# Expert blocks of 128 tokens laid between the tiles of a top-k attention

## Chip, cores and metric

One core of one Trainium2 chip. The metric is the device time of one execution in microseconds; lower is better.

## What is computed

The first stage is attention over 8 batches, 8 heads, 576 positions and head size 64, in which every query keeps only its 32 best scores. Its output, 4608 tokens of 512 numbers, goes through a layer of 8 experts, of which each token uses one. Everything is float32.

```python
scores = scale * np.matmul(q, k.transpose(0, 1, 3, 2))        # (8, 8, 576, 576)
kth = np.partition(scores, -top_k, axis=-1)[..., -top_k:-top_k + 1]
scores = np.where(scores >= kth, scores, -1000000000.0)
attn = softmax(scores)                                        # top_k = 32
x = np.matmul(attn, v).transpose(0, 2, 1, 3).reshape(4608, 512)
logits = x @ w_gate                                           # (4608, 8)
expert_idx = np.argmax(logits, axis=1)
gate_w = probs[np.arange(N), expert_idx]                      # softmax of logits
y[tokens of e] = np.maximum(x[tokens of e] @ w1[e], 0.0) @ w2[e]   # 512 -> 1024 -> 512
out = gate_w[:, None] * y
```

## The kernel before

**Attention.** The work list (`work`) runs over 8 batches, 4 units a batch (a unit is two heads, 128 rows of transposed q and k) and 5 groups a unit: 160 groups. A group is two tiles of 128 queries, one of each head (groups 0 to 3), or one tile that holds the last 64 queries of both heads (group 4); a unit has 9 tiles. For a tile TensorE makes 576 scores per query (`scores`, L213), ScalarE copies them to `s` (L219), and VectorE finds the 32 largest (`weights`): it folds the row into 288 maxima and 288 minima (`hl`, L223 and L224), runs MAX8 four times with three MATCH_REPLACE8 between them over the maxima and MAX8 once over the minima, and merges both into a threshold. GpSimd makes the bias of the exponential (`nbias`, L247), ScalarE the exponential (L249), and VectorE the masked weights `w` and their row sum (L277). `transposed` turns `w` (TensorE L289, L290; ScalarE copies L294, L295); after group 4 `outputs` multiplies by v (L321), turns the result and scales it into `x` (VectorE L330, L337). Groups are software pipelined: scores of group n+1 are issued ahead of the weights of group n, and those ahead of the transposes of group n-1. Within that the framework's scheduler sets each engine's order when the program is built; at run time every engine takes its instructions strictly in that order.

**Routing.** After each second batch `route` works on its 1152 tokens: it turns all of `x` (L350, ScalarE copy L352), multiplies by the gate weights (L354), takes the best expert with small VectorE operations, counts each token's place in its expert's list by two matmuls (L370, L371), scatters token numbers into the lists in DRAM by nine indirect DMAs from GpSimd's queue (L393), each of which waits for the one before, and writes `x` to `x_rows` in DRAM.

**Experts.** After all attention `table` lays the lists out as 25 slots of 256 tokens (18 full ones and up to 7 more, since each expert's last slot is partly empty). A new set of pools is opened. For a slot `load_slot` reads the token numbers and 4 MB of weights (L155, L157; three buffers, two slots ahead) and gathers 256 rows of `x_rows` on GpSimd's queue (L470); `block` turns them (TensorE L482, VectorE copy L483), multiplies by w1 (L488: 128-column weights of TensorE, 256 tokens streaming), applies the rectifier on ScalarE (L491), multiplies by w2 (L495: 512 columns streaming), scales on VectorE (L499) and scatters the rows to the output (L500). In the trace one float32 matmul of the source is two TensorE instructions, each with its own weight load (PEld); a transpose is one.

PSUM has 8 banks: in the attention 4 for scores, 2 for `wTm`, 1 for `wTl` and `xtr`, 1 for `po`, `px`, `pl`, `lg`, `rank`. At the end a run-time branch repeats everything by an exact method if a query's threshold is in doubt; it is not taken here.

Of the kernel before, what the change touches and what calls it, by code (L numbers as in the profile page):

```python
# [26 lines left out]

def _back(ap: bass.AP) -> bass.AP:
# [6 lines left out]
def _inner(ap: bass.AP, n: int) -> bass.AP:  # L35
    return _ins(ap, len(ap.ap), n)


@with_exitstack
def kernel(  # L40
    ctx: ExitStack,
    tc: tile.TileContext,
    qt: bass.AP,
    kt: bass.AP,
    vt: bass.AP,
# [25 lines left out]

    nc = tc.nc
    B, HD, S = qt.shape
# [3 lines left out]
    P = 128  # L77
    D = 64
    U = HD // P
# [6 lines left out]
    NP = B // 2  # L86
# [3 lines left out]
    BLK = 256  # L90
    CB = BLK // P
    EB = N // BLK
    NSLOT = EB + E - 1
    LIST = E * N
    assert ST == 64 and Dm == HD and N == B * S and B % 2 == 0
    assert N % BLK == 0 and LIST % P == 0 and TOP_K == 32 and Dm == 512
    scale = float(D) ** -0.5

# [4 lines left out]
    lists = dram.tile([LIST, 1], I32, name="lists")  # L103
# [10 lines left out]
    nc.sync.dma_start(wg, moe_w_gate.rearrange("(t p) e -> p t e", p=P))  # L114

# [9 lines left out]
    blocks = iota_f("blocks", [1, EB], [[BLK, EB]])  # L125
    slots = iota_f("slots", [1, NSLOT], [[1, NSLOT]])

    def token_ids(t, p):
        b0 = 2 * p * S
        nc.gpsimd.iota(t[:, 0:NC], pattern=[[P, NC]], base=b0, channel_multiplier=1)  # L130
        nc.gpsimd.iota(t[:, NC:2 * NC], pattern=[[P, NC]], base=b0 + S, channel_multiplier=1)
        nc.gpsimd.iota(t[0:ST, 2 * NC:NT], pattern=[[1, 1]], base=b0 + SM, channel_multiplier=1)
        nc.gpsimd.iota(t[ST:P, 2 * NC:NT], pattern=[[1, 1]], base=b0 + S + SM, channel_multiplier=1)

    tok_id = []
    for p in range(NP):
# [12 lines left out]

    w1v = moe_w1.rearrange("e (dt p) f -> p e dt f", p=P)  # L150
    w2v = moe_w2.rearrange("e (ft p) d -> p e ft d", p=P)

    def load_w(pool, e):
        w1 = pool.tile([P, 1, DT, F], F32, name="w1")
        nc.sync.dma_start(w1, w1v[:, bass.ds(e, 1), :, :])  # L155
        w2 = pool.tile([P, 1, FT, Dm], F32, name="w2")
        nc.sync.dma_start(w2, w2v[:, bass.ds(e, 1), :, :])  # L157
        return w1, w2

    firstp = ctx.enter_context(tc.tile_pool(name="firstp", bufs=1))  # L160
# [3 lines left out]
    qk, vs_of, xt, units = {}, {}, {}, {}  # L164

    def open_pools(st, load_bufs, exact):
        for name, bufs in (
            ("load", load_bufs), ("att", 2), ("wtp", 2), ("xp", 1), ("small", 3),
        ):
            setattr(k, name, st.enter_context(tc.tile_pool(name=name, bufs=bufs)))  # L170
        for name, bufs in (("ps_s", 2), ("ps_w", 2), ("ps_1", 1)):
# [3 lines left out]
        k.cnt = None  # L175
        k.ntop = 0
        k.late = None

    def load_qk(b, u, at=None):
        at = b if at is None else at  # L180
        qb = k.load.tile([P, 2, S], F32, name="qb")
        nc.sync.dma_start(qb, qt[at, u * P:(u + 2) * P, :].rearrange("(u p) s -> p u s", p=P))
        kb = k.load.tile([P, 2, S], F32, name="kb")
        nc.sync.dma_start(kb, kt[at, u * P:(u + 2) * P, :].rearrange("(u p) s -> p u s", p=P))
        for n in range(2):
            qk[b, u + n] = (qb[:, n, :], kb[:, n, :])

    def load_v(b, at=None):
        at = b if at is None else at
        vb = k.load.tile([P, KC, HD], F32, name="vb")  # L190
        nc.sync.dma_start(vb[:, 0:NC, :], vt[at, 0:SM, :].rearrange("(c p) d -> p c d", p=P))
        nc.sync.dma_start(vb[0:ST, NC, :], vt[at, SM:S, :])
        vs_of[b] = vb
# [8 lines left out]
    def scores(b, u, tiles):  # L202
        qu, ku = qk[b, u]
# [6 lines left out]
        for j in range(2):  # L210
            for ps, h, rows, cols in todo:
                d = slice(h * D, (h + 1) * D)
                nc.tensor.matmul(  # L213
                    ps[rows, j, 0:HF], qu[d, cols], ku[d, j * HF:(j + 1) * HF], start=True, stop=True
                )
        out_s = []
        for ps in got:
            s = k.att.tile([P, 2, HF], F32, name="s", bufs=4)
            nc.scalar.copy(s, ps[:, :, 0:HF])  # L219
            hl = None  # L220
            if not k.exact:
                hl = k.att.tile([P, 2, HF], F32, name="hl", bufs=4)
                nc.vector.tensor_tensor(hl[:, 0, :], s[:, 0, :], s[:, 1, :], op=ALU.max)  # L223
                nc.vector.tensor_tensor(hl[:, 1, :], s[:, 0, :], s[:, 1, :], op=ALU.min)  # L224
            out_s.append((s, hl))
        return out_s

    def weights(b, u, tiles, ss):
        n = len(tiles)
        s = [a[:, :, :].rearrange("p j k -> p (j k)") for a, _ in ss]  # L230
        tops = tops_of[k.ntop % NTOP]
        k.ntop += 1
        nbias = k.small.tile([P, 2], F32, name="nbias")
        ex = [k.att.tile([P, S], F32, name="ex", bufs=4) for _ in tiles]
        if k.exact:
            src = list(s)
            width = S
        else:
            src = [hl[:, 0, :] for _, hl in ss]
            width = HF  # L240
        scr = [k.att.tile([P, width], F32, name="scr", bufs=3) for _ in tiles]
        R = TOP_K // 8
        for r in range(R):
            for m in range(n):
                nc.vector.max(out=tops[:, m, r * 8:(r + 1) * 8], in_=src[m])  # L245
            if r == 0:
                nc.gpsimd.tensor_scalar(nbias[:, 0:n], tops[:, 0:n, 0], -scale, None, ALU.mult)  # L247
                for m in range(n):
                    nc.scalar.activation(ex[m], s[m], AF.Exp, scale=scale, bias=nbias[:, m:m + 1])  # L249
                if not k.exact:  # L250
                    for m in range(n):
                        nc.vector.max(out=tops[:, m, TOP_K + 1:TOP_K + 9], in_=ss[m][1][:, 1, :])
            if r < R - 1:
                for m in range(n):
                    nc.vector.match_replace(  # L255
                        out=scr[m], in_to_replace=tops[:, m, r * 8:(r + 1) * 8],
                        in_values=src[m], imm_value=NEG,
                    )
                    src[m] = scr[m]
        z = units[b, u][2]  # L260
        i = tiles[0]
        c = 2 * NC if i == 2 * NC else 2 * i
        if k.exact:
            thr = tops[:, :, TOP_K - 1]
        else:
            both = k.small.tile([P, 2, 9], F32, name="both")
            nc.vector.tensor_tensor(
                both[:, 0:n, :], _back(tops[:, 0:n, TOP_K - 9:TOP_K]), tops[:, 0:n, TOP_K:TOP_K + 9], op=ALU.min
            )
            thr = k.small.tile([P, 2], F32, name="thr")  # L270
            nc.vector.tensor_reduce(thr[:, 0:n], both[:, 0:n, :], axis=AX.X, op=ALU.max)  # L271
            over = units[b, u][3]
            nc.gpsimd.tensor_tensor(over[:, c:c + n], tops[:, 0:n, TOP_K + 8], thr[:, 0:n], op=ALU.subtract)
        ws = []
        for m in range(n):
# [372 lines left out]
```

## Time and profile before

| | |
|---|---|
| time, median of 3 runs | 2424.38 us (2403.55 to 2433.43) |
| time of the profiled execution | 2420.5 us, span 2418.8 us |
| TensorE, VectorE, ScalarE, GpSimd busy | 74%, 61%, 29%, 11% of the span |
| granted TensorE clock, mean | 0.785 |
| DMA traffic | 167.0 MB |

The span falls into two stages. In the first, VectorE is nearly always busy and TensorE is busy about two thirds of the time at a clock that changes between its two levels; in the second TensorE is busy all the time at full clock and VectorE hardly at all. Busy times of TensorE include the drain of each matmul, so a high share is not peak use.

### The profile page before, as it was taken

The numbers are of one execution on the slowest core, as the hardware profiler recorded it, in microseconds if no ns is written. First come the engines' busy times: TensorE is split into PE (matmuls) and PEld (weight loads), VectorE is DVE, ScalarE is ACT, GpSimd is POOL, SyncE is SP. The second block draws the span as 40 slices with busy tenths as digits, with TensorE's granted clock in tenths as the row PEclk, the third lists the DMA queues.
The fourth block names the chain that finished last, engine by engine and source line by source line (L and its number), as shares of the span: only waits on it lengthen the run. The fifth ranks groups of instructions, "written<-read, shape, count | busy, mean of one in ns | idle before, by whom it ended". The sixth has DMA issues, their size and how long they took to land. (4 is left out here: it accounts for less than half of the span.)

```text
span 2418.8 us, 23413 instructions
## 1 busy us (share of the span) xinstructions
PE 1781.4 (74%) x7210; PEld 1099.0 (45%) x7210; DVE 1487.1 (61%) x5087; ACT 694.8 (29%) x1457; POOL 257.2 (11%) x486
## 2 busy tenths in 40 slices
PE   5756667666666765666775666662999999999998
PEld 3333335333333533333543333342666666666665
DVE  8899988799999699999769998930000010011000
ACT  3333434344344344443333433410111111111110
POOL 1011000200000011000011100002111111111110
PEclk9677766667766667676657767655999999999999
DMA  4001001100000200100110000014454544445530
GB/s 151 20 2 38 20 1 40 40 20 20 20 20 20 59 21 1 40 21 0 40 40 20 20 1 0 1 39 166 175 174 177 188 172 170 172 172 177 176 127 2
DMA packets 71191, 167.00 MB, mean 69 GB/s; under 512 B 9612, under 2 KB 9740, under 8 KB 71058
## 3 DMA queue, kind: packets, MB, share of 16 engines
q1 hardware_dynamic: 61906, 142.83, 17.6%
q0 software_dynamic: 9152, 22.60, 2.4%
q8 instruction: 59, 0.97, 0.2%
q14 instruction: 74, 0.61, 0.1%
HBM read 146.34 MB, written 22.73 MB: 70 GB/s over the span
## 5 line engine op out<-in xcount | busy, mean ns | idle before, releaser
L289 PE MATMUL wTm<-ident,w 128*128 128x128 f32 x1152 | 265.7, 374 | 492.9 <-DVE w L277 490.6
L289 PEld LDWEIGHTS wTm<-ident,w 128*128 128x128 f32 x1152 | 194.8, 196 | 568.4 <-issue 541.9
L213 PE MATMUL sc<-kb,qb 64*128 64x288 f32 (+1 forms) x1280 | 401.7, 586 | 42.9 <-ACT s L219 35.8
L249 ACT ACTIVATE ex<-s,nbias 128x576 f32<-128x576 f32 x288 | 209.6, 769 | 602.0 <-POOL nbias L247 602.0
L488 PE MATMUL ph<-xTs,w 128*128 128x256 f32 x1600 | 352.7, 381 | 14.1 <-DVE xTs L483 14.1
L245 DVE MAX8 tops<-scr 128x8 f32<-128x288 f32 x864 | 354.4, 446 | 0.1
L495 PE MATMUL py<-w,hT 128*128 128x512 f32 x800 | 347.4, 592 | 0.0
L488 PEld LDWEIGHTS ph<-xTs,w 128*128 128x128 f32 x1600 | 302.6, 190 | 60.0 <-DVE xTs L483 19.8
L499 DVE TENSOR_SCALAR y<-py,xg 128x512 f32<-128x512 f32 x50 | 37.5, 751 | 451.1 <-PE py L495 451.1
L491 ACT ACTIVATE hT<-ph 128x256 f32<-128x256 f32 x200 | 76.6, 383 | 699.7 <-PE ph L488 638.0
L213 PEld LDWEIGHTS sc<-kb,qb 64*128 64x128 f32 (+1 forms) x1280 | 185.8, 238 | 175.1 <-issue 96.8
L255 DVE MATCH_REPLACE8 scr<-tops,scr 128x288 f32<-128x288 f32 x576 | 251.4, 442 | 0.0
L495 PEld LDWEIGHTS py<-w,hT 128*128 128x128 f32 x800 | 152.0, 190 | 180.6 <-issue 179.4
L277 DVE SCALAR_TENSOR_TENSOR w<-s,thr,ex 128x576 f32<-128x576 f32 x288 | 224.0, 809 | 0.4
L321 PE MATMUL po<-wT,vb 128*64 128x288 f32 x1024 | 205.8, 564 | 0.5 <-ACT wT L297 0.5
L219 ACT COPY s<-sc 128x576 f32<-128x576 f32 x288 | 174.6, 633 | 55.4 <-DVE w L277 39.3
L223 DVE TENSOR_TENSOR hl<-s 128x288 f32<-128x288 f32 x288 | 130.3, 452 | 79.2 <-ACT s L219 75.0
L294 ACT COPY wT<-wTm 128x512 f32<-128x512 f32 x256 | 150.5, 588 | 28.7 <-PE wTm L289 27.5
L467 DVE TENSOR_SCALAR src<-idx 128x2 int32<-128x2 int32 x25 | 4.2, 169 | 250.7 <-DMA idx<-lists 250.7
L321 PEld LDWEIGHTS po<-wT,vb 128*64 128x64 f32 x1024 | 92.5, 188 | 118.3 <-issue 77.6
L247 POOL TENSOR_SCALAR nbias<-tops 128x2 f32<-128x2 f32 (+1 forms) x160 | 47.7, 298 | 818.5 <-DVE thr L271 440.4
L224 DVE TENSOR_TENSOR hl<-s 128x288 f32<-128x288 f32 x288 | 129.6, 450 | 0.0
(103 smaller groups left out, 1495.4 us busy)
## 6 DMA issues: line engine op xcount, KB each, us to landing
w<-in_moe_w_dram SPq DMA_DIRECT2D x50, 2048.0 KB, 11.0
qb<-in_qt_dram SPq DMA_DIRECT2D x16, 576.0 KB, 4.1
kb<-in_kt_dram SPq DMA_DIRECT2D x16, 576.0 KB, 5.2
x_rows<-x SPq DMA_DIRECT2D x8, 1026.0 KB, 10.0
vb<-in_vt_dram SPq DMA_DIRECT2D x8, 1024.0 KB, 5.6
x_rows<-x SPq DMA_DIRECT2D x8, 128.2 KB, 10.0
vb<-in_vt_dram SPq DMA_DIRECT2D x8, 128.0 KB, 5.5
xg<-x_rows,src POOLq DMA_INDIRECT x50, 7.0
```

The source lines that it names most:

```text
L213: nc.tensor.matmul(ps[rows, j, 0:HF], qu[d, cols], ku[d, j * HF:(j + 1) * HF], start=True, stop=True)
L219: nc.scalar.copy(s, ps[:, :, 0:HF])
L223: nc.vector.tensor_tensor(hl[:, 0, :], s[:, 0, :], s[:, 1, :], op=ALU.max)
L245: nc.vector.max(out=tops[:, m, r * 8:(r + 1) * 8], in_=src[m])
L249: nc.scalar.activation(ex[m], s[m], AF.Exp, scale=scale, bias=nbias[:, m:m + 1])
L255: nc.vector.match_replace(out=scr[m], in_to_replace=tops[:, m, r * 8:(r + 1) * 8], in_values=src[m], imm_value=NEG,)
L277: nc.vector.scalar_tensor_tensor(out=w, in0=s[m], scalar=thr[:, m:m + 1], in1=ex[m], op0=ALU.is_ge, op1=ALU.mult, accum_out=z[:, c + m:c + ...
L289: nc.tensor.transpose(pm[:, c, :], w[:, c * P:(c + 1) * P], ident)
L294: nc.scalar.copy(wT[:, :, h, q], pm)
L321: nc.tensor.matmul(po[rows, 0:HF], lhsT, rhs, start=(c == 0), stop=(c == KC - 1))
L488: nc.tensor.matmul(ph, w1[:, 0, dt, f * P:(f + 1) * P], xT[:, dt, :], start=(dt == 0), stop=(dt == DT - 1))
L495: nc.tensor.matmul(py, hT[:, f, c * P:(c + 1) * P], w2[:, 0, f, :], start=(f == 0), stop=(f == FT - 1))
```

## The change

- A block is 128 tokens instead of 256: 36 full blocks and up to 7 more, 43 in all, each with its own 4 MB of weights (two buffers).
- `route` runs after every batch (576 tokens, five scatters). `table` runs after every batch from the second on, and hands out as many full blocks as must exist whatever the routing is: 2, 4, 5, 4, 5, 4 after batches 1 to 6 (`sure`), and the remaining 19 after batch 7, the last.
- `block` is a generator of 17 pieces, each of 4 w1 matmuls or 1 w2 matmul; `pieces` lays the blocks of a batch evenly over groups 5 to 19 of the next batch. The 19 blocks of the last batch come after the attention.
- Gate logits are no longer made by turning `x`: `outputs` multiplies each unit's output by its slice of the gate weights (L332), and VectorE scales and adds (three small operations a unit).
- One set of pools for both stages. PSUM: 4 banks for scores, 2 (`ps_t`) for all transposes, outputs and ranks, 2 (`ps_m`) for the blocks.
- The two tiles of a group share one `hl` operation (576 elements instead of two of 288) and one tail copy; the exponential is written into `w` directly.
- The copies of a block (`xTs`, the scaled `y`) go to ScalarE instead of VectorE.
- q and k of a unit come in one DMA, v in one more; unwritten rows of `x_rows` are zeroed at the start.

```diff
-    BLK = 256
...
+    sure = [max(0, -((E * (P - 1) - S * (b + 1)) // P)) for b in range(B - 1)] + [NSLOT]
...
-        for name, bufs in (("ps_s", 2), ("ps_w", 2), ("ps_1", 1)):
+        for name, bufs in (("ps_s", 2), ("ps_t", 2), ("ps_m", 2)):
...
+            hl = k.att.tile([P, 2, 2, HF], F32, name="hl")
+            nc.vector.tensor_tensor(hl[:, 0, m2, :], s[:, m2, 0, :], s[:, m2, 1, :], op=ALU.max)
+            nc.vector.tensor_tensor(hl[:, 1, m2, :], s[:, m2, 0, :], s[:, m2, 1, :], op=ALU.min)
...
+        for t in range(KC):
+            nc.tensor.matmul(
+                pl[:, P + t * lw:P + (t + 1) * lw], oT[:, t * P:(t + 1) * P],
+                wg2[:, n.u, :, :].rearrange("p h e -> p (h e)"), start=True, stop=True,
+            )
...
+    def load_block(expert, piece):
...
+        n.idx = k.mlp.tile([P, 1, 1], I32, name="idx", bufs=3)
+        nc.sync.dma_start(n.idx, lv[:, bass.ds(r, 1), :])
+        n.w1 = k.wp.tile([P, 1, DT, F], F32, name="w1")
+        nc.sync.dma_start(n.w1, w1v[:, bass.ds(e, 1), :, :])
+        n.w2 = k.wp.tile([P, 1, FT, Dm], F32, name="w2")
+        nc.sync.dma_start(n.w2, w2v[:, bass.ds(e, 1), :, :])
...
+    def block(n):
+
+        ps = k.ps_m.tile([P, DT, P], F32, name="xtp", tag="m")
+        for dt in range(DT):
+            nc.tensor.transpose(ps[:, dt, :], n.x[:, dt * P:(dt + 1) * P], ident)
+        xT = k.mlp.tile([P, DT, P], F32, name="xTs")
+        nc.scalar.copy(xT, ps)
+        yield
...
+            ph = k.ps_m.tile([P, FT // 2, P], F32, name="ph", tag="m")
+            for f in range(FT // 2):
+                fc = half * (FT // 2) + f
+                for dt in range(DT):
+                    nc.tensor.matmul(
+                        ph[:, f, :], n.w1[:, 0, dt, fc * P:(fc + 1) * P], xT[:, dt, :],
+                        start=(dt == 0), stop=(dt == DT - 1),
+                    )
...
+                yield
+        py = k.ps_m.tile([P, Dm], F32, name="py", tag="m")
...
+            nc.tensor.matmul(py, hT[:, f, :], n.w2[:, 0, f, :], start=(f == 0), stop=(f == FT - 1))
...
+        nc.scalar.activation(y, py, AF.Copy, scale=n.x[:, Dm:XW])
...
+    PIECES = 2 + 2 * FT - 1
...
+        def ahead():
+            while waiting and len(loaded) < 2:
+                loaded.append(load_block(*waiting.pop(0)))
...
+            new = sure[b] - (sure[b - 1] if b else 0)
+            if new:
+                slot_i = table(new, b == B - 1)
...
+            if at >= 5:
+                pieces(-(-left // (per_batch - at)))
         close(last)
...
+        pieces(left)
```

The order of the instructions, where the prediction speaks of it. TensorE inside the attention, between the scores (`sc`) of neighbouring groups; `px`, `pl` belong to a finished unit, `wTm` and `wTl` are transposes of weights. Before:

```order
L329 MATMUL px<-ident,oT 128x128 x4
L289 MATMUL wTm<-ident,w 128x128 x4
L290 MATMUL wTl<-ident,w 64x128
L289 MATMUL wTm<-ident,w 128x128 x4
L336 MATMUL pl<-ident,oT 64x128
L213 MATMUL sc<-kb,qb 128x288
L290 MATMUL wTl<-ident,w 64x128
L213 MATMUL sc<-kb,qb 128x288 x3
```

The same place now, in the fourth batch; `ph` and `py` are a block's products with w1 and w2 (one row entry is two TensorE instructions), `xtp` the transposes of the next block's rows:

```order
L332 MATMUL pl<-wg_73,oT_113 128x16 x5
L473 MATMUL ph<-xTs,w_4426 128x128 x4
L283 MATMUL wTm<-ident,w 128x128 x8
L473 MATMUL ph<-xTs,w_4426 128x128
L291 MATMUL wTl<-ident,w 64x128 x2
L473 MATMUL ph<-xTs,w_4426 128x128 x8
L482 MATMUL py<-w_4428,hT 128x512
L211 MATMUL sc<-qkb 128x288 x4
L482 MATMUL py<-w_4428,hT 128x512 x2
L283 MATMUL wTm<-ident,w 128x128 x8
```

Block matmuls now stand ahead of scores and transposes in the one queue of TensorE.

TensorE at the end of the attention, before: the logits of the last two batches, the ranks, then the slots.

```order
L350 MATMUL xtr<-ident,x 128x128 x4
L354 MATMUL lg<-wg,xT 128x8 x4
L370 MATMUL rank<-oh,before 128x72
L371 MATMUL rank<-oh,ones 128x72
L556 MATMUL pd<-ones,any_p 1x1
L482 MATMUL xtp<-ident,xg 128x128 x12
L488 MATMUL ph<-xTs,w_1547 128x256 x32
L495 MATMUL py<-w_1549,hT 128x512 x16
```

And now; this row of four repeats for 19 blocks:

```order
L329 MATMUL pl<-ident,oT_117 128x128
L332 MATMUL pl<-wg_73,oT_117 128x16 x5
L362 MATMUL rank<-oh,before 128x40
L363 MATMUL rank<-oh,ones 128x40
L580 MATMUL pd<-ones,any_p 1x1
L463 MATMUL xtp<-ident,xg 128x128 x4
L473 MATMUL ph<-xTs,w_12946 128x128 x32
L482 MATMUL py<-w_12948,hT 128x512 x8
L463 MATMUL xtp<-ident,xg 128x128 x4
```

The chain of logit matmuls is gone, and the next block's transposes come only behind the last w2 matmul.

GpSimd's queue behind the routing of the same batch, before (first routing):

```order
L247 TENSOR_SCALAR nbias<-tops_115 128x2
L393 DMA lists<-tok_id_89,posi 36864x1 x3
L273 TENSOR_TENSOR over<-tops_115,thr 128x2
L247 TENSOR_SCALAR nbias<-tops_109 128x1
L393 DMA lists<-tok_id_89,posi 36864x1 x2
L247 TENSOR_SCALAR nbias<-tops_111 128x2
```

Now (fourth batch); `xg` is the gather of a block's rows:

```order
L382 DMA lists<-tok_id_95,posi 42368x1 x3
L265 TENSOR_TENSOR over<-tops_109,thr 128x2
L242 TENSOR_SCALAR nbias<-tops_111 128x2
L453 DMA xg<-x_rows,idx 128x513
L265 TENSOR_TENSOR over<-tops_111,thr 128x2
L242 TENSOR_SCALAR nbias<-tops_105 128x1
```

The biases that the exponential needs now stand behind gathers too.

## Rows read from the trace of the kernel before

**Rows 1.** Page, busy tenths in 40 slices of the span (60.5 us each).

```profile
PE   5756667666666765666775666662999999999998
...
DVE  8899988799999699999769998930000010011000
...
PEclk9677766667766667676657767655999999999999
```

**Rows 2.** Busy time by stretch: window, length, engines' busy us, then clock, DMA share, GB/s.

```profile
500.00:800.00 300.00, 196.51 (x887) 110.40 (x888) 284.89 (x988) 122.89 (x252) 23.89 (x65) 0.70 0.06 20
...
400.00:500.00 100.00, 72.87 (x323) 47.25 (x321) 74.37 (x270) 35.18 (x71) 15.40 (x25) 0.66 0.17 48
800.00:900.00 100.00, 67.54 (x286) 41.16 (x282) 75.44 (x275) 35.24 (x73) 15.49 (x27) 0.66 0.14 36
1200.00:1300.00 100.00, 68.43 (x270) 41.95 (x270) 70.10 (x257) 34.44 (x71) 15.23 (x25) 0.62 0.14 36
0.00:1592.80 1592.80, 1039.29 (x4504) 600.71 (x4504) 1407.79 (x4919) 613.80 (x1249) 149.10 (x377) 0.70 0.08 26
1592.80:1679.70 86.90, 25.60 (x118) 21.84 (x119) 9.06 (x47) 4.36 (x8) 12.64 (x13) 0.52 0.26 78
1680.00:2418.80 738.80, 716.24 (x2588) 476.17 (x2587) 70.16 (x121) 76.62 (x200) 95.46 (x96) 1.00 0.46 161
```

**Rows 3.** Groups by line, VectorE: busy us, mean ns; idle before it, and its releaser.

```profile
L277 DVE SCALAR_TENSOR_TENSOR w<-s,thr,ex 128x576 f32<-128x576 f32 x288 | 224.0, 809 | 0.4
...
L223 DVE TENSOR_TENSOR hl<-s 128x288 f32<-128x288 f32 x288 | 130.3, 452 | 79.2 <-ACT s L219 75.0
...
L330 DVE TENSOR_TENSOR x<-px,rz 128x512 f32<-128x512 f32 x32 | 22.1, 692 | 72.5 <-PE px L329 72.5
...
L358 DVE COPY lgs<-lg 128x72 f32<-128x72 f32 x4 | 0.9, 232 | 43.0 <-PE lg L354 43.0
```

**Rows 4.** Timeline of one expert slot: start, length, engine, line, count [idle before].

```profile
1737.27 1.04 PE L482 MATMUL xtp<-ident,xg 128*128 128x128 f32 x8
...
1738.88 14.08 PE L488 MATMUL ph<-xTs,w 128*128 128x256 f32 x64 [0.57 <-DVE xTs L483]
...
1752.79 13.90 PE L495 MATMUL py<-w,hT 128*128 128x512 f32 x32
```

**Rows 5.** Timeline, logit matmuls at the high and at the low clock level.

```profile
403.54 1.95 PE L354 MATMUL lg<-wg,xT 128*128 128x8 f32 x16
...
1606.60 1.88 PE L354 MATMUL lg<-wg,xT 128*128 128x8 f32 x8 [0.73 <-ACT xT L352]
```

**Rows 6.** Timeline between the stages: last output, logits, scatters, list read.

```profile
1592.50 0.28 DVE L337 TENSOR_TENSOR x<-pl,rz 64x128 f32<-64x128 f32 x1 [0.39 <-PE pl L336]
...
1619.18 0.23 DVE L358 COPY lgs<-lg 128x72 f32<-128x72 f32 x1 [26.39 <-PE lg L354]
...
1625.59 1.04 POOL L393 DMA_INDIRECT lists<-tok_id,posi  x1 [42.33 <-DVE end L436]
1636.77 0.97 POOL L393 DMA_INDIRECT lists<-tok_id,posi  x1 [10.14 <-DMA lists<-tok_id,posi]
...
1660.57 0.97 POOL L393 DMA_INDIRECT lists<-tok_id,posi  x1 [2.28 <-DMA lists<-tok_id,posi]
1664.94 0.95 SPq L463 DMA_DIRECT2D idx<-lists  x2
```

**Rows 7.** Busy time by stretch around one weight load, columns as in rows 2.

```profile
1901.00:1903.00 2.00, 2.00 (x6) 0.82 (x5) 0.00 (x0) 0.00 (x0) 0.00 (x0) 1.00 0.99 334
1903.00:1905.00 2.00, 2.00 (x6) 0.89 (x5) 0.00 (x0) 0.00 (x0) 0.00 (x0) 1.00 0.99 406
1905.00:1907.00 2.00, 2.00 (x6) 0.95 (x5) 0.75 (x1) 0.00 (x0) 0.00 (x0) 1.00 0.66 270
```

**Rows 8.** Page, DMA issues: count, KB each, median us from issue to landing.

```profile
w<-in_moe_w_dram SPq DMA_DIRECT2D x50, 2048.0 KB, 11.0
```

**Rows 9.** Timeline, the last output rows of the kernel.

```profile
2410.36 0.75 DVE L499 TENSOR_SCALAR y<-py,xg 128x512 f32<-128x512 f32 x1 [6.12 <-PE py L495]
```

More of the change, by code (lines that the diff above doesn't have):

```diff
@@ L76 @@
     F = moe_w1.shape[2]
[L77 to L79 removed]
+    D = P // 2
     NC = 4
@@ L174, in open_pools, with bank, load_unit, open_unit @@
         k.exact = exact
[L175 to L193, printed above, removed]
+        k.unit = 0
+        k.top = 0
+    def bank(name):
+        return k.ps_t.tile([P, SM], F32, name=name, tag="t")
+    def load_unit(b, u):
+        n = SimpleNamespace(u=u)
+        qkb = k.load.tile([P, 2, S], F32, name="qkb")
+        nc.sync.dma_start(qkb, qk[b, u, :, :, :])
+        n.q, n.k = qkb[:, 0, :], qkb[:, 1, :]
+        n.v = k.load.tile([P, KC, P], F32, name="vb")
+        nc.sync.dma_start(n.v, v[b, u, :, :].rearrange("(c p) d -> p c d", p=P))
+        return n
+    def open_unit(n):
+        n.z = k.small.tile([P, NT], F32, name="z")
+        n.over = None if k.exact else k.small.tile([P, NT], F32, name="over")
     def parts(i):
@@ L213, in scores @@
                 nc.tensor.matmul(
-                    ps[rows, j, 0:HF], qu[d, cols], ku[d, j * HF:(j + 1) * HF], start=True, stop=True
+                    ps[rows, j, 0:HF], n.q[d, cols], n.k[d, j * HF:(j + 1) * HF], start=True, stop=True
                 )
[L216 to L234, printed above, removed]
+        s = k.att.tile([P, 2, 2, HF], F32, name="s")
+        for m, ps in enumerate(got):
+            nc.scalar.copy(s[:, m, :, :], ps[:, :, 0:HF])
+        return s
@@ L267, in weights @@
             nc.vector.tensor_tensor(
-                both[:, 0:n, :], _back(tops[:, 0:n, TOP_K - 9:TOP_K]), tops[:, 0:n, TOP_K:TOP_K + 9], op=ALU.min
+                both[:, m2, :], _back(tops[:, m2, TOP_K - 9:TOP_K]), tops[:, m2, TOP_K:TOP_K + 9], op=ALU.min
             )
[L270 to L273, printed above, removed]
@@ L371, in route @@
-        nc.tensor.matmul(rp[:, 1, 0:NT * E], ones, ohf, start=True, stop=True)
-        base = k.small.tile([P, NT + 1, E], F32, name="base", bufs=2)
-        if k.cnt is None:
-            nc.vector.memset(base[:, 0, :], 0.0)
-        else:
-            nc.vector.tensor_copy(base[:, 0, :], k.cnt)
-        for i in range(NT):
+        nc.tensor.matmul(rp[:, 0:KC * E], before, ohf, start=True, stop=True)
+        nc.tensor.matmul(rp[:, 256:256 + KC * E], ones, ohf, start=True, stop=True)
+        base = k.small.tile([P, KC, E], F32, name="base")
@@ L599 @@
-            with ExitStack() as st2:
-                open_moe(st2, 1)
-                at = st2.enter_context(tc.tile_pool(name="at", bufs=1))
-                with tc.For_i(0, NSLOT, 1) as j:
-                    now = at.tile([1, 2], I32, name="now")
-                    for n in range(2):
-                        nc.sync.dma_start(now[:, n:n + 1], slot_d[bass.ds(j + n * NSLOT, 1), :])
-                    block(*load_slot(now[0:1, 0:1], now[0:1, 1:2]))
+            with tc.For_i(0, B, 1) as b:
+                x = k.xp.tile([P, KC, XW], F32, name="x")
+                lg = k.small.tile([P, KC, E], F32, name="lg")
+                for u in range(U):
+                    n = load_unit(b, u)
+                    open_unit(n)
+                    for g in groups:
+                        transposed(n, g, weights(n, g, scores(n, g)))
+                    outputs(n, x, lg)
+                route(x, lg, ids, b * S)
+                nc.vector.tensor_scalar_add(ids, ids, S)
@@ L609 @@
+            slot_i = table(NSLOT, True)
+            nc.sync.dma_start(slot_d.rearrange("(a n) o -> o a n", a=2), slot_i)
+            with tc.For_i(0, NSLOT, 1) as j:
+                now = keep.tile([1, 2], I32, name="now")
+                for n in range(2):
+                    nc.sync.dma_start(now[:, n:n + 1], slot_d[bass.ds(j + n * NSLOT, 1), :])
+                for _ in block(load_block(now[0:1, 0:1], now[0:1, 1:2])):
+                    pass
 _OUTS = [((4608, 512), 'float32')]
```

554 lines of the change are left out of this document (268 added, 286 removed).

## Prediction, made before the result was known

> **What bounds the kernel now.** I read the slices of the page first, then the busy time by stretch, the groups by line, and the timelines of single places. The slices show two stages that use opposite engines [rows 1]: for some 26 of 40 slices VectorE stands at 8 to 9 tenths and TensorE at 5 to 7, then TensorE at 9 and VectorE near nothing. In numbers [rows 2]: up to 1592.8 us, when the last attention output is written, VectorE is busy 1407.8 us and idle 185.0; 86.9 us follow in which nearly everything waits; then 738.8 us of expert slots, with TensorE busy 716.2 us at clock 1.00. The span is the sum, 2418.8 us, and the execution took 2420.5, 1.7 more. So VectorE bounds the first stage, and TensorE the last. In a quiet stretch of the first VectorE is busy 284.9 us of 300; in each of three stretches of 100 us that hold a routing only 70 to 75 [rows 2]. Of its idle time 79.2 us wait for score copies, 72.5 for the transposed outputs and 43.0 for the logits [rows 3].
>
> **The expert work that stays at the end.** The stage of 738.8 us goes, and 19 of 43 blocks stay as a tail. A block has 64 w1 instructions on 128 streamed columns, 16 w2 instructions and 4 transposes. Before, 64 w1 instructions on 256 columns took 14.08 us, less the drain (378 ns of one matmul) some 0.217 each, and 32 w2 instructions 13.90 us, 0.43 each [rows 4]. Half the columns halve the streaming, to about 0.11, but each instruction still loads 128 columns of weights, and that this hides is not shown before. From below: 8 transposes with the same 128 by 128 load and 128 streamed columns took 1.04 us, 0.11 each behind the first [rows 4]. A float32 load with next to nothing to stream, the logit matmul, took 1.95 us for 16, about 0.117 each [rows 5]. If load and streaming did not overlap at all, it would be 0.22. I take 0.115, nearest to both rows: 64 x 0.115 = 7.4 us. The w2 part is 16 x 0.43 = 6.9. Between the last w2 matmul and the next w1 the transposes and a copy stand alone, as before, when 1.6 us passed from the first transpose to the first w1 matmul [rows 4]; two ScalarE operations in a row (y, then xTs) make that no shorter, so 1.6. A block takes 15.9 us, and 19 of them 302.
>
> In the Trainium skill, "TensorE: Matmul & The Clock Gate", section "Back-to-back issue gap", pairs of a weight load and a matmul are spaced by both: at 128 columns about 81 ns where the matmul alone would take 56, 1.45 times as much. By that the 0.11 would become 0.16 and the tail 55 us longer; the transposes above show no such surcharge, the w1 matmuls at 128 columns are not in the trace. That is rival A.
>
> Weights could be late: each block now loads 4.2 MB for half the tokens. One 2.1 MB load keeps the DMA engines at 0.99 for about 4 us and 0.66 for 2, moving 334, 406 and 270 GB/s [rows 7], so about 6 us of transfer; 11.0 us is its median from issue to landing [rows 8]. With two buffers w1 of the block after next is asked for when a block's w1 part ends and is due some 24 us later, w2 likewise; two loads need 12 us and the rows in and out (0.5 MB) 1.5, together 13.5 of 15.9 us. Hidden, with 2.4 us to spare; at 270 GB/s it would be 17.5 us a block and 30 us in all.
>
> **The gap ahead of the tail.** Before, it went: last output 1592.50, logits ready 1619.18, first scatter 1625.59, second 1636.77, ninth 1660.57, list read 1664.94, first w1 matmul 1679.7 [rows 2, 6]. Now the logits come with the outputs (0.8 us for three small operations), the chain to the first scatter stays at 6.4 us, five scatters take 11.2 + 3 x 3.4 + 4.4 = 25.8 (later ones were 3.4 apart), and list read to first matmul stays 14.8, in which the weights (11.0) land as well. That is 48 us for 86.9. Behind the last w2 matmul comes what came before: 8.4 us from the last output scaling to the end of the span [rows 2, 9].
>
> **The attention stage.** VectorE's work in it first. More: four more routings (7 for 3 in this stage) of about 25 operations at 0.2 us (0.23 on 72 columns [rows 3], now 40), 20 us; six tables of some 26 such operations, 31 us, which before came once and behind the stage; three logit operations in each of 32 units, 22 us. Less: 256 folds of 576 elements stand for 512 of 288. A fold of 288 takes 0.45 us [rows 3], some 0.37 from start to start; 576 elements are bounded by half the cost (the fixed part alone merged, -50 us) and by the 0.81 of the masked product on 576 elements [rows 3], no gain; near the latter, I take -19. The copies of a block go to ScalarE, which is idle 60% of the stage [rows 2]; four operations of about 0.6 us a block, 58 us in all, hide there. VectorE: 1407.8 + 54 = 1462.
>
> Its idle time next. The three routing stretches lose about 20 us each against their neighbours [rows 2]; without the logit chain and with five scatters for nine I take 5 for each of seven, bounded by 0 and 20: 185 - 60 + 35 = 160. The end of the stage is then at 1622 us.
>
> That costs the 24 interleaved blocks at nothing, hidden by VectorE, and it is the largest entry of the sum. TensorE is busy 196.5 of 300 us at clock 0.70, so 138 at full clock, or 4.6 us a group (30 groups of 9.95 us) [rows 2]; a block adds 14.8 us without its gap, and 4 or 5 blocks over 15 groups add 3.9 or 4.9. Sum 8.5 to 9.5 us, against 1622 / 160 = 10.1 for a group. It fits, barely, and only at full clock. The clock goes between 1.2 and 2.4 GHz, 0.70 being a mixture; it was 1.00 where TensorE was busy 97% [rows 2], and the fuller queue should hold it higher than before. The 72.5 us that VectorE waits for outputs would shrink with that clock, while two PSUM banks for four, and waits for block data at the head of TensorE's queue, stretch them; I let these cancel. Queued behind a waiting block matmul are the next scores, and VectorE waits for those; behind a waiting gather on GpSimd stand the biases, which ScalarE needs within a group. Gathers are ordered a whole unit after the routing, and scores a group ahead, so waits up to about 10 us vanish.
>
> **Sum.** 1622 + 48 + 302 + 8.4 = 1980 us of span, 1982 with the 1.7; the profiled execution stands 0.2% under the median, which I leave out: 1980.
>
> **The rivals.**
> A, weight loads pace w1: at 0.16 the tail is 19 x 64 x 0.045 = 55 us longer, 2035; at 0.22, 128 longer, 2108. For it, that the load is as long as the stream; against, the transposes.
> B, TensorE's queue paces the interleaved groups: stalls for lists, gathers, weights and ScalarE's copies stand between tiles, and if 90 groups go from 10.1 to 11.4 us, 117 us come back: 2097. For it, the sum of 8.5 to 9.5 us a group; against, that busy time counts drains. It decides from 10.1 us of TensorE a group.
> C, slower: the clock stays at 1.2 GHz between the tiles. The same logit loads then take 0.23 for 0.117 [rows 5], a group 2 x (4.6 + 4) = 17 us on the mean of the 90, 620 us more: 2600. It passes the old time only if these groups lengthen by over 5.5 us each. For it, the 0.70 at 65% busy; against, 1.00 in the slots.
> D, better: at the faster clock VectorE's waits for scores and outputs (152 us [rows 3]) fall by two thirds: 1880.
> E, the overlap doesn't happen: every block stands in VectorE's way for its full 15.9 us, 24 x 15.9 = 382: 2362, 2.6% under before.
>
> **Chances.** The forecast 0.60, by itself 1930 to 2030; A 0.13, B 0.16, D 0.07, C 0.02, E 0.02. The range 1890 to 2110 takes in A and B whole and most of D. 2% is about what a measurement of this kernel can tell from no change; faster by more than that in all but C and half of E: 0.96, within 0.02, slower 0.02.
>
> **What would show it.** Right: the last attention output near 1620 us with VectorE busy about 90% up to there; clock above 0.85 in the second to last batches; 19 blocks 16 us apart behind a gap of about 48; w1 matmuls 0.115 us apart. A shows in that spacing; B in VectorE's idle time, released by score copies, while TensorE waits for gathers or copies; C in the granted clock; late weights in idle TensorE ahead of w1. Wrong: a tail period over 18 us, or an attention stage beyond 1700.

## The result and the profile after

The changed kernel took 1911.66 us (median of four runs), the kernel before 2418.4 beside it: a ratio of 0.7905, 95% interval 0.7853 to 0.7958. The profiled execution has a span of 1909.3 us. The forecast was 1980, its range 1890 to 2110.

The slices of the page, 47.7 us each, answer to [rows 1].

```profile
PE   5778677877886699769996998599969973999998
...
DVE  8999889997999799989997999799988970000000
...
PEclk9765666568956799779985998699959986999999
```

In 33 of the 40 slices both engines are now busy at once. Busy time by stretch, in the columns of [rows 2]: to the last attention output, to the first w1 matmul of the end, to the end.

```profile
0.00:1572.70 1572.70, 1270.90 (x6524) 788.81 (x6524) 1415.16 (x4925) 645.97 (x1192) 179.90 (x428) 0.80 0.32 101
1572.70:1607.86 35.16, 2.28 (x11) 1.73 (x11) 6.17 (x39) 0.82 (x2) 5.82 (x6) 0.51 0.41 127
1607.86:1909.30 301.44, 280.73 (x1592) 202.53 (x1592) 0.00 (x0) 44.30 (x75) 36.94 (x37) 0.99 0.79 282
```

Against [rows 2] the expert stage went from 738.8 to 301.4 us (-437), the gap from 86.9 to 35.2 (-52) and the attention from 1592.8 to 1572.7 (-20): together the 509.5 us that the span lost. TensorE does 232 us more work in the attention and VectorE 7 more, in less time; the clock there rose from 0.70 to 0.80. VectorE's groups, as in [rows 3]:

```profile
L269 DVE SCALAR_TENSOR_TENSOR w<-s,thr,w 128x576 f32<-128x576 f32 x288 | 223.7, 807 | 12.5 <-ACT w L244 11.5 <-DVE rz L305 0.3
...
L232 DVE TENSOR_TENSOR hl<-s 128x576 f32<-128x576 f32 (+1 forms) x160 | 109.5, 685 | 63.9 <-ACT s L216 63.7
...
L324 DVE TENSOR_TENSOR x<-px,rz 128x512 f32<-128x512 f32 x32 | 21.9, 685 | 57.2 <-PE px L322 57.0
```

The wait for score copies fell from 79.2 to 63.9 us and that for outputs from 72.5 to 57.2; new is one of 12.5 for the exponential (0.4 before). The 43.0 for logits are gone, but not all of them were the attention's, as the prediction reads them: 26.4 stood in the gap [rows 6] and 16.6 in the attention. A block of the end on TensorE, the counterpart of [rows 4]:

```profile
1670.21 0.60 PE L463 MATMUL xtp<-ident,xg 128*128 128x128 f32 x4
1671.68 7.41 PE L473 MATMUL ph<-xTs,w 128*128 128x128 f32 x64 [0.87 <-ACT xTs L465]
1678.92 7.03 PE L482 MATMUL py<-w,hT 128*128 128x512 f32 x16
1685.79 0.60 PE L463 MATMUL xtp<-ident,xg 128*128 128x128 f32 x4
```

From xtp to xtp 15.58 us; 64 w1 matmuls start to start in 7.24 us, 0.113 each, and TensorE is idle for 0.87. The gap, on GpSimd, as in [rows 6]: five scatters, then the first gather.

```profile
1578.32 1.05 POOL L382 DMA_INDIRECT lists<-tok_id,posi  x1 [17.56 <-DVE full L413]
1583.54 0.95 POOL L382 DMA_INDIRECT lists<-tok_id,posi  x1 [4.17 <-DMA lists<-tok_id,posi]
...
1594.50 0.90 POOL L382 DMA_INDIRECT lists<-tok_id,posi  x1 [2.40 <-DMA lists<-tok_id,posi]
1599.49 0.99 POOL L453 DMA_INDIRECT xg<-x_rows,idx  x1 [4.08 <-DMA idx<-lists]
```

One new wait comes back once in each of the six batches with blocks: TensorE stands for 7.5 to 8.4 us at the transposes of the batch's first block. The timelines of TensorE, ScalarE and VectorE where the first batch with blocks begins:

```profile
424.67 2.29 PE L211 MATMUL sc<-qkb 64*128 64x288 f32 x4
...
441.46 1.11 PE L463 MATMUL xtp<-ident,xg 128*128 128x128 f32 x4 [7.46 <-DMA xg<-x_rows,idx]
```

```profile
442.62 0.59 ACT L465 COPY xTs<-xtp 128x512 f32<-128x512 f32 x1 [8.21 <-PE xtp L463]
443.10 0.78 ACT L244 ACTIVATE w<-s,nbias 128x576 f32<-128x576 f32 x1
443.77 0.58 ACT L286 COPY wT<-wTm 128x512 f32<-128x512 f32 x1
444.24 1.19 ACT L216 COPY s<-sc 128x576 f32<-128x576 f32 x2
```

```profile
445.46 0.76 DVE L232 TENSOR_TENSOR hl<-s 128x576 f32<-128x576 f32 x1 [9.85 <-ACT s L216]
```

TensorE stood for 7.46 us, as the block's gather had not landed. The scores that VectorE needed next were done at 427, but on ScalarE their copy stands behind xTs, w and wT, and xTs and wT need TensorE's transposes: VectorE waited 9.85 us. The same is seen at 644, 837 and 1230 us (10.2, 8.8, 9.4); in the other two batches it waits for scores 2.9 to 3.4 us at a time and then 6.2 and 5.6 us for outputs.

### The profile page after: what moved, and what is told of

Same layout as the page of the kernel before. It is cut to its first block, busy times and chain, and to the rows that moved or that the text cites. A ratio compares the mean times of both kernels' runs of the same rounds, so it can differ in the third digit from the quotient of the medians.

```text
span 1909.3 us, 25156 instructions
## 1 busy us (share of the span) xinstructions
PE 1553.9 (81%) x8126; PEld 993.1 (52%) x8126; DVE 1421.3 (74%) x4963; ACT 691.1 (36%) x1269; POOL 222.7 (12%) x471
## 4 chain that ended last, share of the span: by engine, by line
DVE 45%; PE 26%; DMA 14%; issue 10%; ACT 3%; POOL 2%; SPq 0%; POOLq 0%; DVEq 0%; ACTq 0%
DVE tops L240 13%; DVE scr L250 12%; PE po L317 9%; DVE w L269 7%; DMA out_dram<-y,idx 7%; PE sc L211 5%; PE ph L473 4%; DVE hl L232 3%; DVE tops L247 3%; DVE hl L233 3%; DMA idx<-lists 3%; DMA lists<-tok_id,posi 2%; DMA xg<-x_rows,idx 2%; PE wTm L283 2%; PE py L482 2%
## 5 line engine op out<-in xcount | busy, mean ns | idle before, releaser
L211 PE MATMUL sc<-qkb 64*128 64x288 f32 (+1 forms) x1280 | 379.5, 545 | 9.6 <-DMA qkb<-in_qk_dram 5.7
L473 PE MATMUL ph<-xTs,w 128*128 128x128 f32 x2752 | 348.2, 283 | 27.7 <-ACT xTs L465 27.4
L244 ACT ACTIVATE w<-s,nbias 128x576 f32<-128x576 f32 x288 | 211.9, 773 | 229.4 <-POOL nbias L242 228.7
L211 PEld LDWEIGHTS sc<-qkb 64*128 64x128 f32 (+1 forms) x1280 | 179.7, 221 | 130.2 <-issue 62.0
L269 DVE SCALAR_TENSOR_TENSOR w<-s,thr,w 128x576 f32<-128x576 f32 x288 | 223.7, 807 | 12.5 <-ACT w L244 11.5
L317 PE MATMUL po<-wT,vb 128*64 128x288 f32 x1024 | 158.5, 458 | 1.1 <-ACT wT L288 0.9
L232 DVE TENSOR_TENSOR hl<-s 128x576 f32<-128x576 f32 (+1 forms) x160 | 109.5, 685 | 63.9 <-ACT s L216 63.7
L240 DVE MAX8 tops<-hl 128x8 f32<-128x288 f32 x288 | 126.0, 448 | 0.0
L250 DVE MATCH_REPLACE8 scr<-tops,hl 128x288 f32<-128x288 f32 x288 | 125.7, 440 | 0.0
L291 PE MATMUL wTl<-ident,w 128*64 128x128 f32 x288 | 76.3, 347 | 55.3 <-ACT wT L286 54.6
L247 DVE MAX8 tops<-hl 128x8 f32<-128x288 f32 x288 | 120.6, 444 | 0.0
```

What stands on the lines that cost most here:

```text
L211: nc.tensor.matmul(ps[rows, j, 0:HF], n.q[d, cols], n.k[d, j * HF:(j + 1) * HF], start=True, stop=True)
L232: nc.vector.tensor_tensor(hl[:, 0, m2, :], s[:, m2, 0, :], s[:, m2, 1, :], op=ALU.max)
L244: nc.scalar.activation(w[:, m, :], flat[m], AF.Exp, scale=scale, bias=nbias[:, m:m + 1])
L247: nc.vector.max(out=tops[:, m, TOP_K + 1:TOP_K + 9], in_=hl[:, 1, m, :])
L250: nc.vector.match_replace(out=scr[:, m, :], in_to_replace=tops[:, m, r * 8:(r + 1) * 8], in_values=src[m], imm_value=NEG,)
L269: nc.vector.scalar_tensor_tensor(out=w[:, m, :], in0=flat[m], scalar=thr[:, m:m + 1], in1=w[:, m, :], op0=ALU.is_ge, op1=ALU.mult, accum_o ...
```

## The experiments

Before took 2422 to 2429 us beside these runs, and the ratios' intervals are about 0.005 to each side (12 us). Two executions with one order of rows up to the end of the attention differed by 13 us there (the last experiment but one), so a difference of 13 us or less between two attention ends shows nothing by itself; busy times, waits and periods are read finer.

**All blocks at the end.** `sure = [0] * (B - 1) + [NSLOT]` in place of the guaranteed counts, and without the zeroing of x_rows that only early gathers need.

> All 43 blocks come after the attention, none between its tiles; the zeroing of unwritten rows goes too. Theory 1 (VectorE bounds the attention and hides the 24 blocks, but for the waits at each batch's first block): the attention ends 40 to 60 us earlier, at 1515 to 1535, the gap stays 35, the tail is 43 x 15.55 = 669, the end 8: about 2240. Theory 2 (the blocks between the tiles cost the attention a good part of their own 370 us): the attention ends below 1450 and the whole is under 2170. Theory 3 (the faster clock that the blocks bring is worth more than they cost): the attention ends later than 1573, the whole is over 2285.

```profile
0.00:1557.70 1557.70, 1137.28 (x4508) 636.91 (x4508) 1404.07 (x4818) 591.15 (x1096) 119.35 (x380) 0.63 0.09 25
1594.70:2277.70 683.00, 636.43 (x3612) 459.19 (x3612) 0.00 (x0) 101.50 (x172) 84.36 (x85) 0.99 0.82 292
```

2277.23 us, ratio 0.9391 (0.9324 to 0.9457). The windows show the attention ending at 1557.7, 15 us sooner than with blocks, and, 37 us later, 43 blocks. So 24 blocks that take 24 x 15.58 = 374 us at the end cost some 10 to 15 between the tiles, and laying them there is worth 2277 - 1912 = 365 of the 507 us. Of the 15 us, 11 are VectorE's work (1415.16 for 1404.07 us, 107 operations more, since the tables that hand the blocks out fall away here) and only 4 its idle time. Why so little, VectorE's waits show:

```profile
DVE x L324 <- PE px L322: 92.4, 32, 10.1
...
DVE hl L232 <- ACT s L216: 12.5, 8, 4.8
```

Columns: total us, times, longest. Without blocks the clock is 0.63 and the outputs are waited for longer (92.4 us against 57.0), as are the exponentials (23.1 against 11.5), the scores less (12.5 against 63.7). So the blocks add 51 us of waiting for scores, most of it the stalls above, and take 47 off the other two waits, with the clock at 0.80. No theory's numbers were met: the attention's end lies between those of theories 1 and 3. Theory 2 is out; the blocks are nearly hidden, as theory 1 says, and of theory 3 it is true that something is paid back, not that it is more than the blocks cost.

**One fold per tile.** `for m in m_all:` around the max and the min, so two operations on 288 columns in place of one on 576.

> The fold of a group's two tiles as two operations of 288 again instead of one of 576; nothing else. Theory 1 (VectorE bounds the attention, and the small operations of routing and tables cost half of what I put on them): 256 times two starts of 0.37 us for one of 0.67, 18 us more, all of it in the time: 1930. Theory 2 (merging the folds saved far more than the 19 us of the prediction, which is why VectorE's busy time came out 47 us lower): 45 to 65 us more, 1957 to 1977. Theory 3 (TensorE paces the groups): no change, 1912.

```profile
0.00:1590.80 1590.80, 1251.98 (x6524) 772.71 (x6524) 1429.07 (x5182) 640.63 (x1192) 191.44 (x428) 0.81 0.33 100
```

1932.96 us, ratio 0.7971 (0.7917 to 0.8024). VectorE is busy 1429.07 us for 1415.16: the merged folds are worth 14 us of VectorE's work, where the forecast had 19. The time is 21 us longer, 16 by the ratios, near theory 1 and far from theory 2, though the intervals overlap. So the forecast's error in VectorE's sum lies elsewhere.

**The first block of a batch later.** Its four transposes stand behind the scores that follow.

```diff
+        with tc.issue_after(k.sc.ins) if k.first else nullcontext():
+            for dt in range(DT):
+                nc.tensor.transpose(ps[:, dt, :], ...
```

> The transposes of each batch's first block are ordered behind the scores of the group after next, so that the gather has some 13 us more; the last batch is left alone. Theory 1 (six waits of TensorE for the gather, 47 us, hold up the scores and VectorE for 8.8 to 10.2 us each): these waits go and the time falls by 35 to 50 us, 1862 to 1877. Theory 2 (VectorE would have waited anyway, or the blocks that move later now press on the groups behind): under 10 us, 1902 to 1920.

```profile
DVE x L325 <- PE px L323: 53.2, 19, 8.8
DVE hl L233 <- ACT s L217: 34.6, 15, 4.7
DVE w L270 <- ACT w L245: 22.5, 8, 6.1
```

1896.8 us, ratio 0.7822 (0.7769 to 0.7874). TensorE's waits for the gather in the attention fell from 47.1 to 0.6 us, VectorE's wait for scores from 63.7 to 34.6 and its longest from 10.2 to 4.7: the early transposes were the cause of the long ones. 11 us came back as waits for the exponentials (22.5 against 11.5). The time is 15 us less, 20 by the ratios, between the two theories.

**The next block's transposes ahead of w2.** turn(nxt), with the xtp transposes and the copy, stands before the w2 matmuls of the block in front of it.

> The next block's transposes and their copy come ahead of a block's w2 matmuls instead of behind them. Theory 1 (TensorE bounds the tail, and 1.3 us of each 15.55 is the wait for the copy): 18 x 1.3 = 23 us less, 1888, period 14.3 us. Theory 2 (the weights' DMA, busy 79% there, holds the period): under 8 us less, and TensorE waits ahead of w1 for weights.

```profile
1749.15 0.63 PE L463 MATMUL xtp<-ident,xg 128*128 128x128 f32 x4 [1.10 <-DMA xg<-x_rows,idx]
```

```profile
1741.95 0.98 POOL L454 DMA_INDIRECT xg<-x_rows,idx  x1 [15.97 <-ACT y L494]
```

1924.26 us, ratio 0.7935 (0.7882 to 0.7988): no gain. The timelines show why neither theory held. w1 now starts right behind w2, but with two xg buffers the gather is issued only when y has released one (1741.95, behind <-ACT y), and the transposes, now due half a block sooner, wait for it at every block: from the first xtp of the end to the last instruction 321.9 us pass, 303.2 before.

**The same, with three xg buffers** (`bufs=3`, idx 4).

> The next block's transposes and copy stand ahead of the w2 matmuls, as in the run before, and xg has three buffers in place of two (idx four). Theory 1 (the gather's buffer made every block wait there): TensorE's waits of xtp for xg go but for the first, and the period at the end falls from 15.55 by the 0.86 us that w1 waited for xTs, to 14.7: 19 x 14.7 = 279 in place of 301, attention end 1564, in all 1880 to 1892 us. Theory 2 (the weights' DMAs hold the pace as soon as it is shorter: 4.7 MB in 14.7 us are 320 GB/s against 282 now): a period of 15.4 or more, w1 or w2 waiting for its weights, 1902 us or more.

```profile
1747.76 0.60 PE L463 MATMUL xtp<-ident,xg 128*128 128x128 f32 x4
1748.61 7.13 PE L490 MATMUL py<-w,hT 128*128 128x512 f32 x16 [0.25 <-ACT hT L484]
...
1762.72 0.60 PE L463 MATMUL xtp<-ident,xg 128*128 128x128 f32 x4
```

1897.8 us, ratio 0.785 (0.7808 to 0.7892). The period is 14.96 us: the wait for the gather is gone, as theory 1 had it, and 0.25 for hT is new. No w1 waits for its weights, so their DMAs carry this pace. The second to fourth blocks of the end still waited 1.2 to 2.8 us for xg, so the end as a whole took hardly less (300.7 us for 303.2). The total falls between the theories, but its 14 us are not the ones that theory 1 looked for: 13 of them lie in the attention (last rank matmul 1562.7 for 1575.5), where so much shows nothing by itself.

**Both edits together.**

> The run above and the later first block of a batch together. Theory 1 (they act at different places, one on VectorE's waits in the attention, the other on the pace at the end): the 19 us of attention and the 16 of the end add up, 1870 to 1884 us. Theory 2 (the early turn frees TensorE only to move the same waits): within 6 us of the better of the two alone.

1882.15 us, ratio 0.7782 (0.7738 to 0.7826), within theory 1's numbers, but not by its parts: the end took 303.9 us, no less than before, and all 30 us lie in the attention (last rank matmul 1545.4 for 1575.5). That the pace at the end added its 16 us is not shown.

**One more MAX8 per group**, `nc.vector.max(out=tops[:, 0, TOP_K + 1:TOP_K + 9], in_=hl[:, 1, 0, :])`, overwritten at once.

> One more MAX8 over 288 columns per group on VectorE, 160 x 0.363 = 58 us. Theory 1 (VectorE bounds the attention also with the blocks between): 45 to 62 us longer, 1957 to 1974, VectorE's idle time within 15 of the 157 of the changed kernel. Rival B (TensorE's queue paces the groups that have blocks in them, 15 of 20 per batch in seven batches): VectorE has room there, and only the groups without blocks pay, under 30 us.

```profile
0.00:1605.00 1605.00, 1278.22 (x6524) 783.75 (x6524) 1464.81 (x5085) 646.99 (x1192) 178.08 (x428) 0.79 0.32 99
```

1943.72 us, ratio 0.8037 (0.7982 to 0.8092). VectorE is busy 50 us more, and 32 show. Neither theory's number was met: VectorE's idle time fell from 157 to 140, so a third of what is added to VectorE goes into its waits.

**w1 twice between the tiles.** Every w1 matmul of the 24 blocks is issued twice, which doubles its result.

> Every w1 matmul of the blocks that lie between the attention tiles is issued twice (their w1 result is doubled); the blocks at the end are as they were. 24 x 64 = 1536 instructions more at 0.113 us, 174 us of TensorE. Theory 1 (VectorE bounds, TensorE has 0.6 to 1.6 us to spare in a group of 10.1 us): 14 or 15 more per group take 1.6 to 1.7 us, of which at most 1.1 stick out, on some 105 groups: 20 to 110 us longer, 1932 to 2022. Rival B (TensorE's queue is the pace already): all of it sticks out, 150 us or more, 2062 or above. Under 20 us would show that TensorE has more to spare than its busy time says.

```profile
0.00:1650.00 1650.00, 1401.92 (x8054) 938.05 (x8054) 1434.03 (x4924) 650.45 (x1192) 171.17 (x428) 0.84 0.31 97
```

```profile
DVE hl L233 <- ACT s L217: 131.9, 43, 10.1
```

1991.51 us, ratio 0.8234 (0.8177 to 0.8291): 80 us for 1536 x 0.113 = 174 us of TensorE. Theory 1 holds, rival B doesn't: more than half of it was hidden. What stuck out is VectorE's wait for score copies, 131.9 us against 63.7. The groups with blocks are 90 in six batches, not the 105 in seven that this expectation and the one before count with.

**The idx reads ahead of the weights**, up to four blocks ahead on SP's queue.

```diff
+            while waiting and len(indexed) + len(loaded) < 4:
+                indexed.append(load_index(*waiting.pop(0)))
+            while indexed and len(loaded) < 2:
+                loaded.append(load_block(indexed.pop(0)))
```

> On top of the run with both edits: the idx reads go on SP's queue up to four blocks ahead, in front of the weights of the blocks before, in place of one by one behind them. Theory 1 (the gathers of the first blocks at the end were late because their idx stood behind 2-MB loads on SP's queue: the second idx landed 12 us late): the waits of 0.87, 2.73 and 2.96 us for xg in the first blocks at the end go, 5 to 9 us less, 1873 to 1877. Theory 2 (the gather itself is slow while weights load, 7 us for 257 KB): the waits stay, within 2 us of 1882.

1902.58 us, ratio 0.7825 (0.7776 to 0.7873). The end did what theory 1 said, 293.4 us from its first xtp against 303.9, but the time did not: the last rank matmul came at 1572.6 for 1545.4. TensorE's rows in the attention came out in another order; that this is the cause is not shown.

**Two blocks held back for the gap**, on top of that.

> On top of that: two of the last batch's blocks are kept out of the attention and stand on TensorE's queue right behind the last rank matmul, in the 31 us in which it waited for the last lists. Theory 1 (a block between the attention tiles is not quite free: 0.46 of TensorE's added time showed in the run with w1 twice): 2 x 15 us x 0.46 = 14 us less in the attention, the gap covered, and the end begins at the full clock: 10 to 22 us less than the run above. Theory 2 (they were free where they lay, 24 blocks cost 15 us in all): 1 to 5 us less. Theory 3: the tail's first weights wait for the two blocks' buffers, and the time stays or grows.

1905.43 us, ratio 0.7845 (0.7794 to 0.7895). The two blocks stood in the gap, and the attention got no shorter for it (last rank matmul 1574.4). That is nearest to theory 2, they had been free; but the 14 us of theory 1 are no more than two like attentions differ by, so it is not excluded.

**The idx reads ahead at the end alone**, with the order of the attention that "both edits" has.

> The run with both edits, with the idx reads ahead of the weights for the 19 blocks of the end alone; TensorE's and VectorE's rows stand in the same order as in that run. Theory 1 (idx in front of the weights took the waits of the first blocks at the end, and what the run with it everywhere lost came from the other order of its attention): from the first xtp of the end to the last instruction 293 to 295 us in place of 304, attention within 4 us of that run, 1869 to 1877 us. Theory 2 (the idx reads ahead cost the attention itself, or put off the weights): within 3 us of 1882, or more.

Transposes of the second to fourth block of the end, with both edits, and then with the idx reads ahead as well:

```profile
1589.64 0.63 PE L465 MATMUL xtp<-ident,xg 128*128 128x128 f32 x4 [0.87 <-DMA xg<-x_rows,idx]
1607.02 0.63 PE L465 MATMUL xtp<-ident,xg 128*128 128x128 f32 x4 [2.73 <-DMA xg<-x_rows,idx]
1626.31 1.08 PE L465 MATMUL xtp<-ident,xg 128*128 128x128 f32 x4 [2.96 <-DMA xg<-x_rows,idx]
```

```profile
1605.07 0.60 PE L476 MATMUL xtp<-ident,xg 128*128 128x128 f32 x4
1620.04 0.60 PE L476 MATMUL xtp<-ident,xg 128*128 128x128 f32 x4
1635.00 0.60 PE L476 MATMUL xtp<-ident,xg 128*128 128x128 f32 x4
```

1886.7 us, ratio 0.7755 (0.7721 to 0.779). The waits are gone and the end takes 293.9 us, 10 less. The attention, with the same order of rows on every engine, ended 13 us later than in the other run (last rank matmul 1558.7). So the total lies where theory 2 has it, yet not for its reason, since the runs part long before the first early idx read, at the first outputs, with both edits and then here:

```profile
65.01 0.69 DVE L325 TENSOR_TENSOR x<-px,rz 128x512 f32<-128x512 f32 x1 [1.48 <-PE px L323]
```

```profile
66.39 0.69 DVE L326 TENSOR_TENSOR x<-px,rz 128x512 f32<-128x512 f32 x1 [2.80 <-PE px L324]
```

The first 16 products with v ahead of them took TensorE 2.79 us in the one run and 4.11 in the other, the next 16 took 2.16 in both. The step is 1.4 us, and others follow up to the 13. Why the same matmuls ran at another pace is open (before took 2422.2 and 2427.8 us beside the two). By the ratios this version and the one with both edits can't be told apart; both beat the changed kernel, by 1.3 to 1.9% as times or ratios are taken.

**Only the copy of the first block later.** In the changed kernel, xTs behind the next score copies on ScalarE, the transposes where they were.

```diff
+        with tc.issue_after(k.sc.ins) if k.first else nullcontext():
+            nc.scalar.copy(xT, ps)
```

> The transposes of a batch's first block stay where they are on TensorE's queue; only their copy xTs on ScalarE (and with it the w1 matmuls) goes behind the copies of the next scores. In the changed kernel the scores were in PSUM at 427 us, and their copy on ScalarE stood behind xTs, w, wT until 444.2. Theory 1 (the copy xTs at the head of ScalarE's queue is what holds up the score copy): the waits of VectorE for s fall as in the run with the transposes later, to 30 to 45 us, the longest under 6, and the time by 10 to 20 us. Theory 2 (wT, also ahead of the score copy on ScalarE, needs TensorE's wTm, which stands behind the block's transposes and their gather: TensorE's queue holds up the score copy through wT): the longest wait stays at 9 to 10 us, the sum over 50, the time within 8 us of 1912.

ScalarE's timeline at the same place:

```profile
446.60 0.59 ACT L287 COPY wT<-wTm 128x512 f32<-128x512 f32 x1 [6.23 <-PE wTm L284]
447.08 1.19 ACT L217 COPY s<-sc 128x576 f32<-128x576 f32 x2
```

```profile
DVE hl L233 <- ACT s L217: 60.6, 17, 10.5
```

1922.56 us, ratio 0.7957 (0.7916 to 0.7999), not told apart from the changed kernel. VectorE's waits for s are 60.6 us, the longest 10.5: theory 2, though the time is 11 us above 1912 and not within 8. With xTs out of the way the score copy stood behind wT, which waited for wTm on TensorE's queue behind the gather. So it is the place of the transposes on TensorE that decides, as the run that moved them showed, and ScalarE's order that passes the stall on.

## Why the prediction was right

The direction, the range and the mechanism held: VectorE bounds the attention and hides nearly all of the 24 blocks. 71 us of the sum did not hold. Part by part: attention 1572.7 for 1622 (-49), gap 35.2 for 48 (-13), 19 blocks 296.3 for 302 (-6), end 5.1 for 8.4 (-3).

**VectorE's sum was mis-sized.** The idle time came out as said (157.5 for 160), the busy time not: 7 us more than before, for 54. The step that failed is "25 operations at 0.2 us", "26 such operations" and the logits, 73 us. The groups of before and after, added up, show 78 small operations of routing with 15.0 us, and 336 of logits, routing and tables with 58.3 (a routing has 20 now, a table 18): 258 more, not 352, of 0.17 us each, so 43 us of durations. And they overlap, here in a routing:

```profile
404.54 0.19 DVE L354 TENSOR_TENSOR oh<-oh,e_less 128x40 f32<-128x40 f32 x1
404.64 0.19 DVE L386 TENSOR_TENSOR lg<-lg,mx 128x40 f32<-128x40 f32 x1
404.76 0.20 DVE L356 TENSOR_REDUCE idx<-oh 128x5 f32<-128x40 f32 x1
```

Each lasts 0.19 and the next begins 0.11 later. VectorE's busy time rose by 7.4 with the folds' 14 taken off, so the small operations cost about 21 us, an estimate. A fold of 576 elements lasts about 0.75 us (0.76 at 445.46 above; the mean of 685 ns is taken together with the folds of 288), near the masked product, as the forecast chose.

**The waits: right sum, other parts.** The forecast had 60 us go with the old routings, 35 come for the new, and let the faster clock and the blocks' stalls cancel. Before, the three stretches with a routing [rows 2] held 51 us of the waiting for scores, here in the first of them (15.9 and 19.4 us in the others):

```profile
DVE hl L223 <- ACT s L219: 15.8, 5, 8.3
```

They went: in the run without blocks the scores are waited for 12.5 us in all. Yet that run leaves VectorE idle for 154 us (1557.7 less 1404.1), with 92.4 for outputs in place of 72.5, and the blocks then add 51 and take 47. That the sum came out at 157.5 for 160 is in part luck. The step that failed is that "waits up to about 10 us vanish", because scores are ordered a group ahead: the scores were ahead, their copy on ScalarE was not.

**The gap.** Five scatters took 16.2 us from first to last, not 21.4: the second came 5.2 us after the first, where the nine before had shown 11.2 [rows 6]; why is open. From the last scatter to w1 13.4 us passed, for 19.2.

**The end.** w1 at 0.113 us for 0.115, a w2 part of 6.9, and 1.47 from the first transpose to w1 for 1.6: 15.58 us for 15.9.

**The rivals.** A fell: 0.113 against 0.16. In the Trainium skill, "TensorE: Matmul & The Clock Gate", section "Back-to-back issue gap", pairs of a weight load and a matmul at 128 columns stand about 81 ns apart where the matmul alone would take 56, 1.45 times as much. For these float32 matmuls this trace does not agree: 0.113 us at 128 columns is 1.04 times half of the 0.217 that 256 columns took. B shows at the first block of a batch and hardly elsewhere; the run with w1 twice shows how near it is, where 174 us more on TensorE let 80 through. C fell: the clock was 0.83 to 0.88 in the 200-us windows from 600 us on, and 0.74 in the one from 400, where the blocks begin. D was right in kind: the two waits fell from 152 to 121 us, a fifth and not two thirds. E fell: some 10 to 15 us, not 382.

## What to carry to other kernels

Work for an idle engine is nearly free between the tiles of a busy one until its queue stands still: look at what the first piece waits for, put it behind the work that the busy engine needs next, and follow that work through the in-order queue of the engine between them. A step moved earlier needs its input earlier; buffers and the queue that brings it have to move along, here the third xg buffer and the idx reads ahead of the weights. Small operations that alternate between independent chains should be priced from start to start, not by their durations.

## What the runs showed of the hardware

Not expected: a faster clock paid back much of the stalls that the blocks brought. Without blocks the attention ran at 0.63 of the full clock, with them at 0.80, and VectorE's waits for outputs were 92.4 and 57.0 us. One unit, the second of the fifth batch, shows how, without blocks and then with them:

```profile
880.00:882.00 2.00, 2.00 (x12) 1.01 (x10) 2.00 (x10) 0.00 (x0) 0.19 (x1) 0.50 0.00 0
```

```profile
888.00:890.00 2.00, 2.00 (x18) 0.97 (x18) 2.00 (x10) 0.00 (x0) 0.00 (x0) 1.00 0.63 254
```

Clock is the third number from the end. Without blocks TensorE had stood idle for 3.9 and 1.8 us shortly before; its chain from the first product with v to px began at 0.50 of the clock and took 8.9 us, and VectorE waited 3.15 us for it. With them the chain ran at 1.00 and took 7.0 us, 1.0 of it a block's matmuls, and VectorE did not wait. That all 35 us have this cause is not shown.

And a small list read behind two 2-MB loads on SP's queue held the second gather of the end for 12.5 us, while the same reads ahead of them let three gathers go out 1.3 us apart. The second gather, with both edits:

```profile
1583.44 0.96 POOL L455 DMA_INDIRECT xg<-x_rows,idx  x1 [12.54 <-DMA idx<-lists]
```
